# Sliding-window attention beside a gated MLP: the band in pieces of 64 queries, with shared columns for the half-masked ends

## The chip, the core and the metric

The kernel runs on one core of one Trainium2 chip. The metric is the device time of an execution in microseconds (us), lower is better; runs of the same kernel agree within a few tenths of a microsecond. The engines are named as in the profile: PE (matmuls), PEld (its weight loads), DVE (vector), ACT (activations), POOL (GpSimd), SP (the engine that issues most DMAs).

## The reference, cut to what matters

```python
x = A_x                                   # 1 x 2048 x 512, bf16
xn = layernorm(x)
# A: attention, 32 heads of 16, each query sees itself and the 255 keys before it
q, k, v = split_heads(xn @ wqkv)          # 512 -> 3 x 32 x 16
mask = (i - j >= 0) & (i - j < 256)
a = softmax(where(mask, q k^T * 16 ** -0.5, -1e9)) v
A = merge_heads(a) @ wo
# B: gated MLP with a mixing over the tokens
z = gelu(xn @ w_in)                       # 512 -> 2 x 688
z1, z2 = z[:, :688], layernorm(z[:, 688:])
g = w_sp @ z2 + b_sp[:, None]             # w_sp is 2048 x 2048
out = x + A + (z1 * g) @ w_out
```

## The kernel before

There are 2048 tokens in 16 row blocks of 128, and 32 heads in 4 groups G of 8. All order is written out by hand: each engine executes its instructions in the order in which the Python emits them.

**Stage one** (to about 54 us) loops over the row blocks. For block n it normalizes x (`stats` on DVE with a power on POOL, `norm` on DVE into the tile xn), transposes xn into `xnT`, and runs two groups of matmuls `do_z` (L285) whose results ACT turns into `z1_all` and `z2_all` with the Gelu (L293); DVE then normalizes z2. The first X_DMA = 8 blocks are transposed on PE (`transpose_x`, L274, with an ACT copy), the others by a DMA that SP issues (L265). From n = 5 on, one projection for head group 0 goes with each block (`early`: k, q and v of token groups 0 to 2, evicted by ACT); the last of them, v of group 2, goes with n = 14. x, w_in, wqkv, wo and w_out are loaded on SP's queue near the start, wo and w_out (L331 to L335) right after the last x block. N_WARM sets how many matmuls on zeros go ahead of the first work on PE.

**The band stage** executes a list of tokens, ORDER, one after the other:
- `pkGg`, `pqGg`, `pvGg` (capital P: another PSUM bank): the projection of head group G for 512 tokens g, on PE, evicted by DVE. k is kept twice, each copy with one half of each pair of heads set to zero (`emask`); a v tile has the layout [v of even heads, ones, v of odd heads], so one matmul gives both the output and the softmax sum.
- `qIIe`: scores of tile II for parity e. The band has 45 blocks of 128 keys x 128 queries for each head group (a key block kb meets query blocks kb, kb+1, kb+2), in the order of key blocks, 4 blocks to a tile: 45 tiles for the 4 groups. For each of the 4 head pairs s, a matmul on 32 rows of the array (32 x 128 tile form) takes the keys as weights and up to 384 queries as moving columns into the bank of strip s (L483). Then ACT takes two exponentials of 128 x 1024 into the tile E (L491), scaled.
- `mII`: masks on E. On blocks with kb = qb POOL's affine_select (L502) drops the keys after the query; on blocks with qb = kb+2 DVE multiplies by `fmask` (L507).
- `aGw`, `AGw` (and the pair `C`, `B`): values. For 256 queries w, 4 matmuls side by side on 32 columns each (128 x 32 tile form, L531) per key block, query block and parity; DVE transposes the result in 32 x 32 blocks, takes the reciprocal of the sums, POOL multiplies (`divide`). `t`: DVE transposes the attention output back (`finish`, L565).
- a number n: n matmuls of the token mixing, w_sp times z2 (`mix`, L402, 512 in all: 16 row blocks x 2 halves x 16 steps), with DVE's product with z1 after each 16. w_sp arrives transposed by DMA, one row block at a time into two buffers (`load_wsp`, L386, on SP's queue; the first two are issued ahead of the token list).
- `o`, `O`: half of a row block's output (L433 for wo, L439 for w_out), a DVE sum, and a DMA to the output, on SP's queue but for the last three blocks, which go on ACT's.

Score tiles, projections with P and outputs with O share three PSUM buffers of two banks (`ps_s`); another bank (`ps_y`) serves projections, values and outputs, and one the mixing. The k, q and v tiles live in rings of NRING = 6, the E tiles in EBUFS = 7 buffers.

## Time and profile before

The runs took 267.82, 267.84 and 267.96 us (median 267.84). The profiled execution took 268.1 us; its span, from the first to the last instruction, is 266.1 us.

| stretch (us) | PE busy | DVE busy | ACT busy | POOL busy |
|---|---|---|---|---|
| 0 to 20 (start of stage one) | 18.0 | 16.2 | 11.7 | 8.2 |
| 20 to 55 (stage one) | 34.7 | 29.4 | 24.9 | 13.6 |
| 55 to 90 (band) | 34.3 | 24.1 | 35.0 | 15.4 |
| 90 to 130 (band) | 39.4 | 31.7 | 39.6 | 22.4 |
| 130 to 170 (band) | 39.7 | 33.2 | 36.6 | 21.5 |
| 170 to 210 (band) | 39.8 | 29.3 | 35.0 | 24.2 |
| 210 to 242 (band, outputs) | 31.6 | 21.6 | 22.6 | 12.8 |
| 242 to 266.1 (mixing, outputs) | 20.9 | 11.7 | 0.5 | 5.4 |

Busy time is the union of an engine's instructions in the stretch. Matmuls overlap one another, so the busy time of PE says that it was never without one, not that the array was full; what an instruction of PE costs is the distance from its start to the next one's. The granted clock is 1.00 in every stretch.

### The profile page before, as it was taken

The numbers are of one execution on the slowest core, as the hardware profiler recorded it, in microseconds if no ns is written. First come the engines' busy times: TensorE is split into PE (matmuls) and PEld (weight loads), VectorE is DVE, ScalarE is ACT, GpSimd is POOL, SyncE is SP. The second block draws the span as 40 slices with busy tenths as digits, with TensorE's granted clock in tenths as the row PEclk, the third lists the DMA queues.
The fourth block names the chain that finished last, engine by engine and source line by source line (L and its number), as shares of the span: only waits on it lengthen the run. The fifth ranks groups of instructions, "written<-read, shape, count | busy, mean of one in ns | idle before, by whom it ended". The sixth has DMA issues, their size and how long they took to land.

```text
span 266.1 us, 8418 instructions
## 1 busy us (share of the span) xinstructions
PE 258.6 (97%) x3661; PEld 147.1 (55%) x3694; DVE 197.3 (74%) x384; ACT 206.0 (77%) x235; POOL 123.6 (46%) x140
## 2 busy tenths in 40 slices
PE   7999999999999999999999999999999999999995
PEld 2565665645455547554656656655665454554543
DVE  5999999567766778968788888767777658568542
ACT  3677767699999999999999899897899789553000
POOL 4334454115645256746637493156573617247200
PEclk9999999999999999999999999999999999999999
DMA  6992325700504050251312054033059972423733
GB/s 204 350 363 55 61 40 112 88 2 2 110 15 98 2 111 21 63 46 38 81 31 52 17 66 81 2 81 83 15 130 272 143 123 59 98 74 30 150 91 89
DMA packets 60132, 23.63 MB, mean 89 GB/s; under 512 B 51216, under 2 KB 59584, under 8 KB 60096
## 3 DMA queue, kind: packets, MB, share of 16 engines
q1 hardware_dynamic: 59472, 22.70, 38.5%
q8 instruction: 29, 0.48, 0.7%
q10 hardware_dynamic: 576, 0.39, 0.5%
q0 software_dynamic: 48, 0.00, 0.3%
q14 instruction: 7, 0.06, 0.1%
HBM read 8.41 MB, written 2.10 MB: 39 GB/s over the span
## 4 chain that ended last, share of the span: by engine, by line
PE 88%; ACT 7%; DMA 2%; issue 1%; SPq 1%; DVE 0%; ACTq 0%
PE gf L402 28%; PE zs L285 14%; PE S L483 11%; PE m L151 8%; PE o_t L531 8%; PE fo L439 8%; ACT E L491 7%; PE m L135 5%; PE fo L433 5%; DMA w_in_sb<-in_B_w_in_dram 2%; PE tp L274 1%; ACT L491 0%; DVE xnT L444 0%; SPq L194 0%; SPq L196 0%
## 5 line engine op out<-in xcount | busy, mean ns | idle before, releaser
L491 ACT ACTIVATE E<-S 128x1024 bf16<-128x1024 f32 x180 | 168.4, 1056 | 18.1 <-PE S L483 14.1
L402 PE MATMUL gf<-z_all,wspT 128*128 128x344 bf16 x512 | 94.2, 310 | 0.0
L502 POOL TENSOR_SCALAR_AFFINE_SELECT E<-E 128x1024 bf16<-128x1024 bf16 x64 | 79.3, 1264 | 18.1 <-ACT E L491 18.0
L402 PEld LDWEIGHTS <-wspT 128*128 128x128 bf16 x512 | 44.2, 98 | 33.8 <-issue 10.5
L554 POOL TENSOR_TENSOR o_norm<-o_c,rsum 128x256 bf16<-128x256 f32 x32 | 23.2, 726 | 77.3 <-DVE rsum L552 77.3
L507 DVE TENSOR_TENSOR E<-E,fmask 128x1024 bf16<-128x1024 bf16 x56 | 51.9, 954 | 1.6 <-ACT E L491 1.5
L285 PE MATMUL zs<-w_in_sb,xnT 128*128 128x176 bf16 (+1 forms) x250 | 39.7, 307 | 0.7 <-DMA w_in_sb<-in_B_w_in_dram 0.4
L483 PE MATMUL S<-q,k 32*128 32x128 bf16 (+2 forms) x888 | 38.5, 251 | 0.8 <-ACT E L491 0.8
L293 ACT ACTIVATE z_all<-zs 128x688 bf16<-128x688 f32 x32 | 23.8, 744 | 12.5 <-PE zs L285 12.5
L151 PE MATMUL m<-xnT,wqkv 128*128 128x512 bf16 x110 | 31.3, 379 | 0.9
L285 PEld LDWEIGHTS <-xnT 128*128 128x128 bf16 x256 | 22.2, 98 | 15.3 <-issue 0.6
L409 DVE SCALAR_TENSOR_TENSOR z_all<-gf,b_all,z_all 128x344 bf16<-128x344 f32 x32 | 18.2, 570 | 15.8 <-PE gf L402 15.7
L483 PEld LDWEIGHTS <-k 32*128 32x128 bf16 x888 | 15.2, 92 | 25.7 <-issue 23.7
L548 DVE STREAM_TRANSPOSE o_c<-o_t 128x512 f32<-128x512 f32 x32 | 22.3, 698 | 8.2 <-PE o_t L531 8.0
L531 PE MATMUL o_t<-E,v 128*32 128x128 bf16 x1440 | 24.5, 220 | 0.0
L531 PEld LDWEIGHTS <-v 128*32 128x32 bf16 x1440 | 20.3, 97 | 6.2 <-issue 6.0
L439 PE MATMUL fo<-w_out_sb,uT 128*128 128x512 bf16 (+2 forms) x98 | 23.0, 366 | 0.3 <-issue 0.2
L444 DVE TENSOR_TENSOR xnT<-fo,xnT 128x512 bf16<-128x512 f32 (+2 forms) x17 | 11.1, 657 | 13.6 <-PE fo L439 13.6
L171 DVE TENSOR_TENSOR k<-m,emask 128x1024 bf16<-128x1024 f32 x13 | 15.8, 1219 | 6.3 <-PE m L151 6.3
L151 PEld LDWEIGHTS <-wqkv 128*128 128x128 bf16 x128 | 12.0, 98 | 11.3 <-issue 0.9
L120 POOL TENSOR_TENSOR rstdx<-rs_v,negh 128x1 f32<-128x1 f32 x16 | 10.3, 646 | 16.1 <-DVE rs_v L119 14.7
L298 DVE BATCH_NORM_STATS2 st<-z_all 128x6 f32<-128x344 bf16 x32 | 14.9, 506 | 3.7 <-ACT z_all L293 3.7
(51 smaller groups left out, 177.4 us busy)
## 6 DMA issues: line engine op xcount, KB each, us to landing
xnT<-in_A_x_dram SPq DMA_DIRECT2D x4, 512.0 KB, 6.4
xs<-in_A_x_dram SPq DMA_DIRECT2D x7, 256.0 KB, 7.5
out_dram<-xnT SPq DMA_DIRECT2D x13, 128.0 KB, 1.7
wqkv<-in_A_wqkv_dram SPq DMA_DIRECT2D x1, 1536.0 KB, 7.2
w_in_sb<-in_B_w_in_dram SPq DMA_DIRECT2D x4, 344.0 KB, 5.1
w_out_sb<-in_B_w_out_dram SPq DMA_DIRECT2D x1, 640.0 KB, 10.4
wo_sb<-in_A_wo_dram SPq DMA_DIRECT2D x1, 512.0 KB, 9.1
xs<-in_A_x_dram SPq DMA_DIRECT2D x2, 128.0 KB, 2.1
```

Of the source, the lines that this page charges most:

```text
L151: nc.tensor.matmul(m, lhsT=wqkv[:, c, w0 : w0 + P], rhs=xnT[:, c, grp * 512 : (grp + 1) * 512], start=(c == 0), stop=(c == NDC - 1),)
L285: nc.tensor.matmul(zp[:, lo:hi], lhsT=xnT[:, c, n * P : (n + 1) * P], rhs=w_in_sb[:, c, f0 + lo : f0 + hi], start=(c == 0), stop=(c == NDC ...
L293: nc.scalar.activation(out=dst[:, n, 0:FH], in_=zp[:, 0:FH], func=ACT.Gelu_apprx_tanh)
L402: nc.tensor.matmul(gf[:, 0:FQ], lhsT=wsp_tiles[n][:, c, :], rhs=z2_all[:, c, lo : lo + FQ], start=(c == 0), stop=(c == NB - 1),)
L439: nc.tensor.matmul(fo[:, c0:c1], lhsT=uT_tiles[n][:, c, :], rhs=w_out_sb[:, c, c0:c1], start=False, stop=(c == NFC - 1),)
L483: nc.tensor.matmul(S[:, h2, j * P : (j + w) * P], lhsT=k_t[(G, kb // 4)][32 * s : 32 * s + 32, e, (kb % 4) * P : (kb % 4 + 1) * P], rhs=q_ ...
L491: nc.scalar.activation(out=E[:, j : j + 3 : 2, 0:nb, :].rearrange("p h b c -> p h (b c)"), in_=tiles[pr][:, :, 0 : nb * P], func=ACT.Exp, ...
L502: nc.gpsimd.affine_select(out=E[:, :, j, :], in_=E[:, :, j, :], pattern=[[0, 8], [1, P]], compare_op=ALU.is_ge, fill=0.0, base=0, channel_ ...
L507: nc.vector.tensor_tensor(out=E[:, :, j, :], in0=E[:, :, j, :], in1=fmask[:].unsqueeze(1).to_broadcast([P, 8, P]), op=ALU.mult,)
L531: nc.tensor.matmul(T[32 * s : 32 * s + 32, e, j * P : (j + 1) * P], lhsT=v_t[(G, kb // 4)][:, kb % 4, s, e : e + 2, :].rearrange("p a d -> ...
L548: nc.vector.transpose(out=C[:, 0 : 32 * DH], in_=Tb)
L554: nc.gpsimd.tensor_tensor(out=o_n[:], in0=c_o.rearrange("p e q d -> p q e d"), in1=rsum[:].rearrange("p e q -> p q e").unsqueeze(3).to_bro ...
```

## The change

The band is cut into pieces of 64 queries. A key block kb of 128 keys now meets queries in 64-query steps u: the steps 2kb+1 to 2kb+4 are pieces "F" (all 128 keys against 64 queries; the first still needs the causal mask, the last the far mask). The two ends of a band, step 2kb, of which only the first 64 keys are seen, and step 2kb+5, of which only the last 64 keys are, are each half of a piece. A piece "C" puts both in the same 64 columns: step 2kb of key block kb on the partitions 0 to 63, and step 2(kb-2)+5 of key block kb-2 on the partitions 64 to 127. That makes 304 pieces for the four head groups, 8 to a tile: 38 score tiles.

- A scores matmul now has 64 keys as weights (32 x 64 tile form): each piece takes 8 matmuls, 4 head pairs s times 2 key halves h; runs of F pieces of one key block go together, up to 256 columns. The loop runs over the pieces first, then s and h.
- The values of a C piece need v with its other half at zero: `w_bufs`, zeroed by POOL in stage one, filled from the v tile by two DMAs on SP's queue for each v projection. The value matmuls take runs of 64 to 192 queries, and only the first of a bank opens the accumulation.
- Masks: POOL's affine_select on 64 columns for the first F piece; DVE products on 64 columns for the last F piece (`fmask`) and for each C piece (`cmask`).
- NRING 6 to 5, EBUFS 7 to 6, X_DMA 8 to 6, N_WARM (9, 3) to (10, 3). The second half of w_in's first part is loaded ahead of the second x block. wo and w_out are loaded after the loop of stage one instead of near the start. In the last block, the first 384 output columns go on SP's queue. The token list is a new one.

```diff
-NRING = 6
-EBUFS = 7
-X_DMA = 8
+NRING = 5
+EBUFS = 6
+X_DMA = 6
-N_WARM = (9, 3)
+N_WARM = (10, 3)
-BLOCKS = [
-    [(G, kb, qb) for kb in range(NB) for qb in range(kb, min(kb + 3, NB))] for G in range(NG)
+PIECES = [
+    (G,) + p
+    for G in range(NG)
+    for kb in range(NB)
+    for p in [("C", kb, 2 * kb)]
+    + [("F", kb, u) for u in range(2 * kb + 1, min(2 * kb + 5, 2 * NB))]
 ]
-TILES = [b[i : i + 4] for b in [sum(BLOCKS, [])] for i in range(0, len(b), 4)]
+TILES = [PIECES[i : i + 8] for i in range(0, len(PIECES), 8)]
...
 ORDER = """
-pq10 Pk03 q000 1 pq03 2 q001 4 pk10 q010 9 m00 q011 pv11 m01 4 q020 4 pk11 q021 8 q030 a00 7
...
+pv03 q000 16 q001 pk03 3 q010 1 m00 8 q011 pq03 4 q020 pv10 m01 3 q021 1 a00 4 q030 8 m02 q031
+pk11 2 m03 2 q040 5 a01 q041 3 Pq12 a02 q050 4 t pk10 t q051 m04 8 q060 pq11 2 t 1 q061 5 pk12
+q070 2 m05 6 q071 a03 Pv11 4 m07 q080 pq10 4 q081 m06 a04 6 q090 4 t 6 m08 q091 a05 4 q100 2 m09
...
@@ proj @@
+            for h in range(2):
+                nc.sync.dma_start(out=wt[64 * h : 64 * h + 64, h], in_=t[64 * h : 64 * h + 64])
...
         load_x(0, split=True)
         load_win(1, 0, 2)
+        load_win(1, 2, 4)
         load_x(1)
-        load_win(1, 2, 4)
...
@@ small_setup @@
             if i < NRING:
                 nc.gpsimd.memset(v_bufs[i][:, :, :, 1, :], 1.0)
+                nc.gpsimd.memset(w_bufs[i][:], 0.0)
...
         for n2 in range(4, NB // 2):
             load_x(n2)
-        nc.sync.dma_start(out=wo_sb[:], in_=A_wo.rearrange("(c p) n -> p c n", p=P))
-        nc.sync.dma_start(
-            out=w_out_sb[:, 0:5, :], in_=B_w_out[0:640, :].rearrange("(c p) n -> p c n", p=P)
-        )
-        nc.sync.dma_start(out=w_out_sb[0 : FH - 5 * P, 5, :], in_=B_w_out[5 * P : FH, :])
...
             do_z(n - 1, 0)
+        nc.sync.dma_start(out=wo_sb[:], in_=A_wo.rearrange("(c p) n -> p c n", p=P))
+        nc.sync.dma_start(
+            out=w_out_sb[:, 0:5, :], in_=B_w_out[0:640, :].rearrange("(c p) n -> p c n", p=P)
+        )
+        nc.sync.dma_start(out=w_out_sb[0 : FH - 5 * P, 5, :], in_=B_w_out[5 * P : FH, :])
...
@@ out_part @@
-        (nc.scalar if n >= NB - 3 else nc.sync).dma_start(
+        (nc.scalar if n >= NB - 3 and c1 == D else nc.sync).dma_start(
...
@@ scores @@
-                for j, G, kb, qb, w in segs:
+        for j, G, kind, kb, u, w in segs:
+            for s in range(4):
+                for h in range(2):
+                    if kind == "F":
+                        ku, qu = 2 * kb + h, u
+                    else:
+                        ku, qu = 2 * (kb - 2 * h if kb >= 2 else kb) + h, u + h
                     nc.tensor.matmul(
-                        S[:, h2, j * P : (j + w) * P],
-                        lhsT=k_t[(G, kb // 4)][32 * s : 32 * s + 32, e, (kb % 4) * P : (kb % 4 + 1) * P],
-                        rhs=q_t[(G, qb // 4)][32 * s : 32 * s + 32, (qb % 4) * P : (qb % 4 + w) * P],
+                        tiles[s // 2][64 * h : 64 * h + 64, s % 2, 64 * j : 64 * (j + w)],
+                        lhsT=k_t[(G, ku // 8)][32 * s : 32 * s + 32, e, (ku % 8) * 64 : (ku % 8 + 1) * 64],
+                        rhs=q_t[(G, qu // 8)][32 * s : 32 * s + 32, (qu % 8) * 64 : (qu % 8 + w) * 64],
                         start=True, stop=True,
                     )
...
@@ masks @@
+            part = E[:, :, 64 * j : 64 * j + 64]
+            if kind == "F" and u == 2 * kb + 1:
                 nc.gpsimd.affine_select(
+                    out=part, in_=part, pattern=[[0, 8], [1, 64]],
+                    compare_op=ALU.is_ge, fill=0.0, base=64, channel_multiplier=-1,
                 )
+            elif kind == "C" or u == 2 * kb + 4:
+                m = cmask if kind == "C" else fmask
                 nc.vector.tensor_tensor(
+                    out=part, in0=part,
+                    in1=m[:].unsqueeze(1).to_broadcast([P, 8, 64]), op=ALU.mult,
                 )
...
@@ values @@
+        steps = [(e,) + tuple(r) for e in range(2) for r in runs(places)]
+        for n, (e, (kind, kb), i, j, u, l) in enumerate(steps):
+            for s in range(4):
+                vt = w_t if kind else v_t
+                vv = vt[(G, kb // 4)][:, kind - 1] if kind else vt[(G, kb // 4)]
+                nc.tensor.matmul(
+                    T[32 * s : 32 * s + 32, e, (u - 4 * w) * 64 : (u - 4 * w + l) * 64],
+                    lhsT=vv[:, kb % 4, s, e : e + 2, :].rearrange("p a d -> p (a d)"),
+                    rhs=E_tiles[i][:, 2 * s + e, 64 * j : 64 * (j + l)],
+                    start=(n == 0), stop=(n == len(steps) - 1), skip_group_check=True,
+                )
```

## The prediction

> **What bounds the kernel now.** I read the page first, for which engine is full and where.

> ```profile
> span 266.1 us, 8418 instructions
> ...
> PE 258.6 (97%) x3661; PEld 147.1 (55%) x3694; DVE 197.3 (74%) x384; ACT 206.0 (77%) x235; POOL 123.6 (46%) x140
> ...
> PE   7999999999999999999999999999999999999995
> ...
> ACT  3677767699999999999999899897899789553000
> ```

> PE is full in every slice between the first and the last; ACT is full only in the first half of the band stage. The list of waits asks whether that full PE ever waits inside:

> ```profile
> PE S L483 <- ACT E L491: 0.8, 3, 0.3
> ```

> Three waits, 0.8 us. So time is PE's own instructions, and the change is first a change in PE's sum. The groups give what it touches:

> ```profile
> L491 ACT ACTIVATE E<-S 128x1024 bf16<-128x1024 f32 x180 | 168.4, 1056 | 18.1 <-PE S L483 14.1
> ...
> L502 POOL TENSOR_SCALAR_AFFINE_SELECT E<-E 128x1024 bf16<-128x1024 bf16 x64 | 79.3, 1264 | 18.1 <-ACT E L491 18.0
> ...
> L507 DVE TENSOR_TENSOR E<-E,fmask 128x1024 bf16<-128x1024 bf16 x56 | 51.9, 954 | 1.6 <-ACT E L491 1.5
> ```

> The mean of a pipelined matmul isn't its price; the distance between starts is. The timeline of PE shows it (start, length, count last):

> ```profile
> 130.13 1.06 PE L135 MATMUL m<-wqkv,xnT 128*128 128x128 bf16 x16
> 131.02 1.04 PE L402 MATMUL gf<-z_all,wspT 128*128 128x344 bf16 x6
> 131.99 0.41 PE L483 MATMUL S<-q,k 32*128 32x128 bf16 x8
> 132.33 0.85 PE L531 MATMUL o_t<-E,v 128*32 128x128 bf16 x48
> 133.13 0.60 PE L402 MATMUL gf<-z_all,wspT 128*128 128x344 bf16 x3
> ```

> Sixteen matmuls of 128 columns take 0.89 us, 0.0556 each; four of 512 (56.14 to 57.00) 0.215 each. So a column costs 0.415 ns and a matmul 2.5 ns more: 0.145 us for 344 columns, 0.029 for 64. Six of 344 from 131.02 end at 131.89, yet the scores start at 131.99: a change of tile form (128*128, 32*128, 128*32) costs 0.10. The 48 value matmuls take 0.80 = 12 sets of four at 0.0556, plus 0.10 for the next change and 0.03; so four strips run together, their weight loads hidden. The scores take 0.34: 512 columns (0.213), two pieces (0.005), a change (0.10), and 0.02 of strips starting in turn. With four pieces it is 0.36 (125.73 to 126.09).

> Last, the start of the band stage, since the order and the queues change there:

> ```profile
> 49.28 0.58 ACT L145 CAST v<-m 128x512 bf16<-128x512 f32 x1 [0.15 <-PE m L135]
> ...
> 53.75 1.89 PE L151 MATMUL m<-xnT,wqkv 128*128 128x512 bf16 x8
> ```

> and SP's queue, at the same place and at the one other place where a transpose stands behind large loads:

> ```profile
> 43.14 5.89 SPq L386 DMA_TRANSPOSE wspT<-in_B_w_sp_dram  x2
> ...
> 196.78 3.39 SPq L578 DMA_DIRECT2D xnT<-in_A_x_dram  x4
> 200.28 6.23 SPq L386 DMA_TRANSPOSE wspT<-in_B_w_sp_dram  x1
> ```

> SP issues the first two w_sp transposes from 43.14; the first lands 4.5 us later, at 47.6, long before the first mix matmul (55.91). At 200.28 a transpose issued behind four 512 KB loads of the same queue is held by them for 6.23 us and lands after 9.8.

> **PE's sum.** Counts come from the instruction order of both kernels. Scores: 90 groups become 76. Columns per strip go from 184320/4 to 311296/8, 46080 to 38912, matmuls per strip from 222 to 352: 19.7 to 17.0 us, −2.65. Form changes fall from 206 to 181: −2.5. The starting of strips: eight instead of four, up to five pieces; I take 0.05 for the 0.03 of now, 76×0.05 against 90×0.03: +1.1 (bounds −1 and rival B). Values: the same columns in 2048 matmuls for 1440, 152 more sets of four at 2.5 ns: +0.4 (0 to rival B). Together −3.65.

> **Stage one.** Two row blocks leave PE's transposes for DMA: 8×0.0556, −0.45. Their DMAs are needed at about 22.6 us; each takes 2.4 us (as the others) from xn written by about 18.3, behind x loads landing until about 19: no wait. w_in's second half goes ahead of the second x load. Now PE waits 0.43 us for w_in at 7.72, and the x block lands at 5.92 (2.20 + 3.7). Swapped, that x lands where w_in lands now, 7.68, 1.75 later. From that x to xn of block 2 takes 2.7 us (5.92 to 8.60), so 10.2, and PE, which now reaches that transpose at 9.47 and otherwise would at 8.9, waits: +0.75 against now (0 to 1.0). The tenth warm-up matmul ends at 5.49 against xn at 5.40: +0.05. The memsets of the w buffers (POOL's 640-element one takes 0.63, so about 1.5 each) fall in POOL's idle time before rstd (15 us); if not, DVE's xn is 2 us ahead. The first 384 output columns of the last block go through SP's queue, so the last transfer no longer queues behind them: −0.15 (0 to −0.4).

> **The queue.** wo and w_out, loaded at 11 to 22 us now, move behind stage one, ahead of the w_sp transposes on SP. So do two copies for each v projection, which wait for ACT's or DVE's copy of v. The last early v projection is evicted at 49.28+0.58 = 49.86, and stage one ends 0.35 later than now (0.75+0.05−0.45), so 50.2. Behind it SP issues two copies, wo, w_out in two parts (0.45 each, as its x loads): the first w_sp transpose cannot be issued before 52.4; now it is at 43.14. It lands at 52.4+4.5 = 56.9 at the earliest. But 1.2 MB stand before it: wo issued at 51.1, data from 1.75 later (the first 128 KB x load: 2.1 to landing, 0.37 of it transfer), at 0.35 MB/us (1.5 MB of wqkv in 4.5 us), done at 56.3. At 200 us the transpose landed at 210.07, 3.4 after the last load (206.66): 59.7. And the new order asks for it sooner: one v projection, one score group, then 16 mix matmuls. Stage one's last matmul ends at 53.75+0.35 = 54.1; +0.89+0.10+0.36 = 55.45. PE is in order, so all of PE stands behind that mix: 59.7−55.45 = **+4.3 us**, at least 56.9−55.45 = 1.4, at most about 5. The second transpose, some 5.3 later (47.6 and 53.0 now), comes at 65; PE needs it at about 69. In an idle spell of over 4 us the clock may fall: the page's PEclk never shows it in the band, but the first nine 128x512 matmuls run at 0.427 each against 0.215 later, 1.9 us lost; that is an end of the range. [...]

> **Other engines.** ACT: 152 exponentials for 180 at 0.936 (168.4/180): 142 us for 168, so PE's 0.8 us of waits mostly goes: −0.5. POOL: 64 masks of half size. DVE gets 120 mask products of 512 elements for 56 of 1024; the row of that line runs from 0.63 to 1.61 us (the long ones beside POOL's masks), mean 0.93. Half is 0.46; I take 0.5 (0.35 to 0.65): 60 us for 52. Per head group DVE then has 10.4 (k, q, v copies) + 15.0 + 11.0 (eight divisions) + 4.6 (mix) = 41 of PE's 43; now 39 of 47. At 95% some of PE's banks come free late: +0.8 (0 to 4).

> The smaller rings (five k, q, v and w buffers, six E tiles) cost nothing where the order emits a projection after the last value group that reads the buffer it takes (Pv11 stands after a02); the mix matmuls between are the cover, and a miss would cost PE one value group, under 1 us.

> **Sum.** −3.65−0.45+0.75+0.05−0.15+4.3−0.5+0.8 = +1.15. The profiled execution took 268.1, 2.0 over its span; 269.25. The median of the runs, 267.84, lies 0.26 lower: 269.0.

> **Rivals.**
> A, faster: the w_sp transpose is there nearly in time. If loads and transpose shared the 16 DMA engines, it would land at 56.9, PE would wait 1.4: 266.1; without any wait 264.7. For: engines do work side by side, and SP's copies are small. Against: the 6.23 us above. It decides from landing at 58 downward. 0.24.
> B, narrow strips are dear: no set in the trace is narrower than 128 columns. If a set of 64 score columns is held up by its next weights, it takes up to the 0.0556 of now instead of 0.029: 1728/8 = 216 sets, +5.7: 274.7; with the values' 392 sets too, +10.4 more; were only four of the eight strips to run together, +17. Against: loads are hidden today at two in the time of one. 0.12. [...]
> C, DVE becomes the bound in the middle (products at 0.65): 120×0.15 = 18 us more, PE waits some 4: 272.2. 0.10.

> **Numbers.** My forecast has 0.54; its own range is 266.8 to 271.5. Within 0.2% (about what a measurement can tell) is ±0.54. From the forecast come 0.05 faster, 0.13 same, 0.36 slower; A gives 0.23 faster and 0.01 same; B and C 0.22 slower. The range takes in A, C and the clock: 265.7 to 272.8.

> **What would show it.** PE's first mix waits on DMA wspT for 3.5 to 5 us near 55; score groups start-to-next 0.36 to 0.38 on PE; no DVE releaser over 1 us in PE's waits; the tail unchanged. It is wrong if w_sp lands before 57, if a score group takes over 0.42, or if PE waits for DVE by several us.

## The result: slower by an eighth, against a forecast of half a per cent

The changed kernel took 301.61 us (median of four runs, 299.72 to 306.35), the kernel before 267.83 beside it: a ratio of 1.1239, 95% interval 1.1187 to 1.129. The forecast was 269.0, with a range to 272.8. The direction was right, the size far off. The profiled execution took 299.72 us. Every ratio here leaves out disturbed executions (of these four, the one of 306.35 us), so it is not quite the quotient of the medians.

The page of the changed kernel, its lines for the span, the engines, PE's slices, the granted clock and the instruction queue:

```profile
span 298.0 us, 13620 instructions
...
PE 266.9 (90%) x6223; PEld 163.7 (55%) x6223; DVE 210.6 (71%) x449; ACT 182.2 (61%) x205; POOL 95.1 (32%) x147
...
PE   8999889659999889897999699979797969799995
...
PEclk9999999959999999999999979999999999999999
...
q8 instruction: 48, 0.79, 1.2%
```

The span grew by 31.9 us. PE's row of nines is gone: its busy time grew by 8 us, its share fell from 97% to 90%. No other engine is fuller than 71%, so nothing else has become the bound. The two counts to look at are x6223 + x6223 instructions on PE (before 3661 + 3694), and 48 packets on queue q8, which carries instructions, of 16 KB each. The page of the kernel before has 29 of them:

```profile
q8 instruction: 29, 0.48, 0.7%
```

The list of waits of the changed kernel names what PE waited for (total, times, longest):

```profile
PE S L520 <- issue: 8.3, 5, 2.5
...
PE o_t L575 <- issue: 6.9, 7, 2.0
...
PE gf L440 <- DMA wspT<-in_B_w_sp_dram: 6.2, 1, 6.2
...
PE zs L323 <- DMA xnT<-xn: 2.3, 2, 1.2
...
PE m L154 <- issue: 2.1, 1, 2.1
...
PE gf L440 <- issue: 0.6, 1, 0.6
```

"issue" means that nothing in the profile released the engine: no semaphore, no DMA of data. PE's timeline shows such a stop in the middle of a score group, 40 matmuls with no wait among them (start, length, count last; in brackets the idle time):

```profile
198.08 0.60 PE L440 MATMUL gf<-z_all,wspT 128*128 128x344 bf16 x3
198.61 0.54 PE L520 MATMUL S<-q,k 32*64 32x128 bf16 x35
201.24 0.28 PE L520 MATMUL S<-q,k 32*64 32x192 bf16 x5 [2.09 <-issue]
...
236.13 0.51 PE L520 MATMUL S<-q,k 32*64 32x64 bf16 x40
236.57 1.05 PE L440 MATMUL gf<-z_all,wspT 128*128 128x344 bf16 x6
```

The gaps were read from the trace's raw rows: 13 of them lose over half a microsecond each, 19.8 us together, the longest 2.7. Count PE's rows (matmuls and weight loads): all 13 come at row 190 of a run of 256, and q8 brings one packet of 16 KB for every 255 to 259 of these rows (7,390 over 29 packets in the kernel before, 12,448 over 48 in the changed one), so that a packet is read here as one such run. At all 13, PE goes on 1.2 to 1.5 us after the end of a q8 packet: at the gap of 201.24 the packet runs from 198.94 to 199.90, at 241.32 from 238.99 to 240.04. In the kernel before, the shortest block of 256 between these rows lasted 4.26 us, 25 of 28 lasted over 6, and no gap stands at any border. In the changed one 23 of 47 blocks last under 3.8 us. All 13 gaps stand behind blocks of 1.3 to 3.6 us and none behind a longer one; of the ten other short blocks, nine lasted 3.4 us or more.

Where the 31.9 us went: 19.8 gaps at these borders; 6.3 the first mix's wait for w_sp; 2.6 the two waits for xnT in stage one; 3.3 at half clock (6.8 us granted at 0.5 from 59.7, of which PE ran 3.2, and 3.4 from 172.3). That is 32.0, so what is left of the change's own sum nearly cancels; this rest was not measured by itself.

The last two lines of that timeline show a second thing: a score group without a stop takes 0.44 us from its start to the next matmul (236.13 to 236.57). The mean over such groups is 0.437, where 0.375 was expected.

### The profile page after: what moved, and what is told of

It reads as the page before. It is cut to its first block, busy times and chain, and to the rows that moved or that the text cites. A ratio compares the mean times of both kernels' runs of the same rounds, so it can differ in the third digit from the quotient of the medians.

```text
span 298.0 us, 13620 instructions
## 1 busy us (share of the span) xinstructions
PE 266.9 (90%) x6223; PEld 163.7 (55%) x6223; DVE 210.6 (71%) x449; ACT 182.2 (61%) x205; POOL 95.1 (32%) x147
## 4 chain that ended last, share of the span: by engine, by line
PE 71%; DVE 14%; issue 7%; DMA 5%; SPq 2%; POOL 0%; ACT 0%; DVEq 0%
PE gf L440 26%; PE S L520 11%; PE m L174 8%; PE o_t L575 8%; PE fo L477 7%; PE fo L471 5%; PE m L154 4%; DVE st L292 3%; DMA wspT<-in_B_w_sp_dram 2%; DVE st L336 2%; DVE xn L298 2%; PE zs L323 2%; DVE E L543 2%; DMA xs<-in_A_x_dram 1%; DVE z_all L342 1%
## 5 line engine op out<-in xcount | busy, mean ns | idle before, releaser
L528 ACT ACTIVATE E<-S 128x1024 bf16<-128x1024 f32 x152 | 145.5, 1024 | 64.2 <-PE S L520 56.3
L440 PEld LDWEIGHTS <-wspT 128*128 128x128 bf16 x512 | 45.5, 99 | 33.9 <-DMA wspT<-in_B_w_sp_dram 6.3
L537 POOL TENSOR_SCALAR_AFFINE_SELECT E<-E 128x512 bf16<-128x512 bf16 x64 | 47.1, 760 | 27.3 <-ACT E L528 27.3
L520 PE MATMUL S<-q,k 32*64 32x64 bf16 (+3 forms) x2816 | 39.5, 217 | 8.3 <-issue 8.3
L520 PEld LDWEIGHTS <-k 32*64 32x64 bf16 x2816 | 27.9, 105 | 30.7 <-issue 29.8
L323 PE MATMUL zs<-w_in_sb,xnT 128*128 128x512 bf16 (+1 forms) x256 | 40.1, 309 | 2.3 <-DMA xnT<-xn 2.3
L543 DVE TENSOR_TENSOR E<-E,cmask 128x512 bf16<-128x512 bf16 x64 | 37.9, 599 | 0.0
L591 DVE STREAM_TRANSPOSE o_c<-o_t 128x512 f32<-128x512 f32 x32 | 22.6, 707 | 17.4 <-PE o_t L575 16.1
L543 DVE TENSOR_TENSOR E<-E,fmask 128x512 bf16<-128x512 bf16 x56 | 30.3, 542 | 0.1
L575 PE MATMUL o_t<-E,v 128*32 128x64 bf16 (+2 forms) x1088 | 23.6, 215 | 4.4 <-issue 4.3
L575 PE MATMUL o_t<-E,w 128*32 128x64 bf16 x960 | 19.0, 193 | 2.6 <-issue 2.6
L154 PE MATMUL m<-wqkv,xnT 128*128 128x128 bf16 x256 | 17.6, 222 | 2.1 <-issue 2.1
```

Of the source, the lines that this page charges most:

```text
L154: nc.tensor.matmul(m[:, j * P : (j + 1) * P], lhsT=xnT[:, c, n * P : (n + 1) * P], rhs=wqkv[:, c, 2 * D + G * P : 2 * D + (G + 1) * P], st ...
L323: nc.tensor.matmul(zp[:, lo:hi], lhsT=xnT[:, c, n * P : (n + 1) * P], rhs=w_in_sb[:, c, f0 + lo : f0 + hi], start=(c == 0), stop=(c == NDC ...
L440: nc.tensor.matmul(gf[:, 0:FQ], lhsT=wsp_tiles[n][:, c, :], rhs=z2_all[:, c, lo : lo + FQ], start=(c == 0), stop=(c == NB - 1),)
L520: nc.tensor.matmul(tiles[s // 2][64 * h : 64 * h + 64, s % 2, 64 * j : 64 * (j + w)], lhsT=k_t[(G, ku // 8)][32 * s : 32 * s + 32, e, (ku ...
L528: nc.scalar.activation(out=E[:, j : j + 3 : 2, :], in_=tiles[pr][:], func=ACT.Exp, scale=SM_SCALE)
L537: nc.gpsimd.affine_select(out=part, in_=part, pattern=[[0, 8], [1, 64]], compare_op=ALU.is_ge, fill=0.0, base=64, channel_multiplier=-1,)
```

## The experiments

Two theories were tested. **One**: PE's instructions come in blocks of 256, a block takes a few microseconds to come, and the change, with 1.7 times the instructions for the same matrix work, runs PE out of them. **Its rivals**: narrow sets are dear in themselves (B of the prediction), or the gaps are waits for other engines or for traffic. Beside that, the three smaller losses were taken apart.

### e1: narrow matmuls in the kernel before

Each score and value matmul is cut to at most 64 columns; nothing else changes.

```diff
@@ scores, inside "for s" @@
-    nc.tensor.matmul(S[:, h2, j * P : (j + w) * P], ...)
+    for c in range(0, w * P, 64):
+        nc.tensor.matmul(S[:, h2, j * P + c : j * P + c + 64], ...)
```

> The kernel before, with each score and value matmul cut into matmuls of 64 columns (same tile forms, same order of tokens, same queues): 7127 matmuls' worth of PE instructions in place of 3695, 14254 rows in place of 7390. Theory 1 (PE's instructions arrive in blocks of 256, some 4 us after the block before is entered, and PE stands at a block's border where 256 instructions last less than that): idle PE marked 'issue' of 1 to 3 us at borders 256 instructions apart, 15 to 35 us in all, 283 to 303 us, although no piece is in the 32 x 64 form and nothing else has changed. Theory 2 (the gaps belong to the new tile form, the w copies or the new order): only the 2.5 ns of each further matmul and the emptying queue, 1 to 5 us more, 269 to 273 us, and no gap of a microsecond marked 'issue'.

Measured: 349.82 us, ratio 1.288 (1.279 to 1.2969), far above the 283 to 303 expected. 31 us lie in 18 gaps at block borders, the longest 5.2. But the edit brought a second effect: with eight narrow pieces of one strip in a row, the four strips overlapped only in part, and a score group took 0.74 where it takes 0.35, some 35 us over 90 groups. And 37.5 us of the profiled execution ran at half clock. So the gaps are there with none of the change's pieces, masks or copies, but the total doesn't isolate them. e5 repairs that. The "emptying queue" of the second theory is the author's assumption; no run shows it.

### e5: the same, with the strips innermost

```diff
-    for pr, h2 (strip s) ... for j, G, kb, qb, w in segs:
+    for j, G, kb, qb, w in segs:
+        for c in range(0, w * P, 64):
+            for s in range(4):
```

> The kernel before, with nothing changed but that every score and value matmul is cut into pieces of 64 columns, the strips innermost: as many columns and as many multiplications as before, about twice the PE instructions (some 14,250 rows for 7,390). Theory one (TensorE's instructions are delivered in blocks of 256, and a block takes 2.5 to 6 us to come, so that it stands where 256 instructions last less): gaps marked issue at block borders of 20 to 40 us in all, 290 to 315 us. Rival (the narrow sets themselves, or the new masks and forms of the change, cost the time, not the number of instructions): no gaps at the borders, score groups of 0.35 to 0.40 us, 268 to 275 us.

Measured: 324.81 us, ratio 1.2092 (1.2016 to 1.2167), beyond the upper end of the expectation. PE's timeline and the waits of e5:

```profile
244.56 0.39 PE L480 MATMUL S<-q,k 32*128 32x64 bf16 x13 [5.48 <-issue]
...
270.27 0.41 PE L480 MATMUL S<-q,k 32*128 32x64 bf16 x32
270.62 0.60 PE L439 MATMUL fo<-w_out_sb,uT 128*128 128x512 bf16 x2
```

```profile
PE S L480 <- issue: 19.1, 11, 5.5
...
PE o_t L528 <- issue: 16.9, 9, 3.8
```

The undisturbed group from 270.27 takes 0.35 us, as before with half as many pieces (0.34 to 0.36): cutting the sets cost the array nothing. All the loss is outside: 41.1 us in 22 gaps, and 27 us in seven spells of half clock beside gaps, up to 13.6 us more. Together that is up to 54.7 of the span's 55.0. Work, columns, masks and loads are those of the kernel before; the number of PE instructions is not, nor is the order of the strips inside a group, which the group of 0.35 us shows to cost nothing. That is theory one, and it excludes the rival that narrow sets are dear in themselves, and any that needs the change's form, masks or copies.

### e8: the supply by itself

1,024 matmuls of 64 columns behind the last output, when no other engine works.

```diff
+    spare = ps_g.tile([P, 512], F32, name="spare", tag="g")
+    for i in range(1024):
+        s = i % 4
+        nc.tensor.matmul(spare[32 * s : 32 * s + 32, 0:64], lhsT=ident[:, 32 * s : 32 * s + 32],
+                         rhs=wo_sb[:, 0, 0:64], start=True, stop=True)
```

> The kernel before with 1,024 matmuls of 64 columns by 32 rows of output added behind its last output (work that nothing reads; 2,048 PE instructions), four strips in turn, no wait among them. It measures the supply by itself, with no other engine at work. If TensorE had its instructions at once they would take 1,024 x 7.3 ns = 7.5 us. Theory one: eight blocks of 256 at 2.5 to 4 us each, one gap in each at a 256 border, 20 to 30 us more than before. Rival (the gaps come from waits for other engines that the trace does not show): 8 to 12 us more, no gaps.

Measured: 293.06 us, ratio 1.0947 (1.0914 to 1.0981), 25 us more, as theory one has it. PE's timeline:

```profile
263.81 2.17 PE L600 MATMUL spare<-wo_sb,ident 128*32 128x64 bf16 x241
268.31 1.22 PE L600 MATMUL spare<-wo_sb,ident 128*32 128x64 bf16 x128 [2.33 <-issue]
272.03 1.90 PE L600 MATMUL spare<-wo_sb,ident 128*32 128x64 bf16 x128 [2.51 <-issue]
...
282.94 1.90 PE L600 MATMUL spare<-wo_sb,ident 128*32 128x64 bf16 x128 [1.56 <-issue]
```

Bursts of 128 matmuls (256 instructions with their weight loads) start every 3.45 to 3.73 us, whether the burst itself takes 1.2 us or, at half clock, 1.9. So the period is set by the delivery, not by PE, with almost no other traffic (0.25 MB in the 27 us from 264 to 291, seven q8 packets for the seven gaps among it). The rows show its parts: the q8 packet starts 0.95 to 1.16 us after PE has entered the block that goes before, takes 0.93 to 1.36, and PE goes on 1.23 to 1.47 us after its end. At the changed kernel's borders the same period (256 instructions and the gap behind them) is 3.1 to 5.8 us, for example 1.31 + 1.86 and 3.07 + 2.70. There the packet starts 0.1 to 3.4 us after the block is entered, and the four gaps of over 2 us stand behind packets that start 2.4 us after it or later; what makes these late is not shown.

### e4: fewer instructions in the change

The F pieces' scores in the 32x128 form (one matmul for 128 keys instead of two for 64); C pieces behind them. 10,656 PE instructions instead of 12,448.

```diff
-        for j, G, kind, kb, u, w in segs:
+        for j, G, kind, kb, u, w in sorted(segs, key=lambda x: x[2] == "C"):
...
+                if kind == "F":
+                    nc.tensor.matmul(tiles[s // 2][:, s % 2, 64 * j : 64 * (j + w)],
+                        lhsT=k_t[...][32 * s : 32 * s + 32, e, (kb % 4) * P : (kb % 4 + 1) * P], ...)
+                    continue
```

> The changed kernel with the scores of the F pieces taken by whole key blocks (32 x 128 form, one matmul where there were two), the C pieces after them in the 32 x 64 form: PE rows fall from 12448 to 10656, and each score group has one more change of form (76 x 0.1 = 7.6 us). Theory 1: score groups fit in the queue again and blocks of 256 last longer: the gaps marked 'issue' fall from 20 us to 5 to 10, groups are not longer than before by more than the 0.1: 290 to 298 us. If the gaps have nothing to do with the number of instructions, they stay at 20 and the change of form adds 5 to 8: 304 to 310 us.

Measured: 287.56, 288.37, 293.11 and 503.15 us, ratio 1.074 (1.0719 to 1.0762) from the first two. The execution of 503.15 us is the profiled one; its matmuls ran at little more than half the speed (0.259 us from one of 344 columns to the next for 0.146, not a third as the next expectation says), its cause is open, and its profile is not used. A further run gave another:

> The kernel of e4 once more, for a profile whose gaps can be read: the first one's profiled execution ran at a third of the speed throughout. Theory one: 10,656 rows for 12,448, gaps at block borders of 8 to 14 us for 20, the F part of a score group 0.16 us or more shorter or no hole in its pairs, about 287 to 291 us.

288.7 us, with these waits:

```profile
PE gf L440 <- DMA wspT<-in_B_w_sp_dram: 6.8, 1, 6.8
PE o_t L580 <- issue: 4.1, 4, 1.9
PE zs L323 <- DMA xnT<-xn: 2.1, 3, 1.3
...
PE S L525 <- issue: 0.9, 1, 0.9
PE gf L440 <- issue: 0.6, 1, 0.6
```

The border gaps fell from 19.8 to 6.2 us, within the 5 to 10 first expected and under the 8 to 14 of the second expectation; the total fell by 13 us; the waits for w_sp and xnT stayed. A score group did not get shorter: F and C parts together take 0.474, since the change of form between them costs its 0.10 (131.89 to 131.99 in the kernel before). So the time was saved by the smaller number of instructions, not by the form. That a score group must fit in a queue, as the first expectation has it, is the author's assumption; no run shows it.

### e2 and e3: the late loads

e2 is the changed kernel with wo and w_out loaded where they were before; e3 is the kernel before with the change's side edits (x blocks 6 and 7 by DMA, ten warm-up matmuls, w_in's second half ahead of the second x block, late wo and w_out, the split output queue) and nothing of the band.

```diff
@@ e2, against the changed kernel @@
         for n2 in range(4, NB // 2): load_x(n2)
+        (the three DMAs of wo and w_out)
...
             do_z(n - 1, 0)
-        (the three DMAs of wo and w_out)
```

> The changed kernel with the loads of wo and w_out back at their old place, right after the x loads. If the 6.4 us for which the first mix waits on the w_sp transpose come from those loads standing ahead of it, the wait falls to 0 to 1.5 us (the transpose still stands behind the last v copy, 50 us) and with it the spell at half clock after it: 6 to 8 us less than the changed kernel, 293 to 295 us. If the v copies alone held the transpose, the wait stays over 3 us: 298 to 301 us. The gaps marked 'issue' stay at some 20 us under either.

Measured: 297.38 us, ratio 1.1113 (1.1065 to 1.1162): 4 us less than the changed kernel, where 6 to 8 were expected. PE's waits in e2:

```profile
PE zs L323 <- DMA xnT<-xn: 2.7, 1, 2.7
...
PE gf L440 <- DMA wspT<-in_B_w_sp_dram: 0.8, 1, 0.8
```

The wait for w_sp fell from 6.3 to 1.0 us (0.8 in the list, which leaves out the change of form), so the late loads are its cause. But the waits for xnT did not get smaller: in place of the two of 2.6 us in all stands one of 2.9 at 24.9 us, since the DMA transposes of x blocks 6 and 7 now stood behind those loads, and a wait of 0.7 for xn stands at 9.8 us. The gaps (19.1) stayed.

> The kernel before with the side edits alone (6 blocks transposed on PE for 8, ten warm-up matmuls, w_in's second half ahead of the second x block, wo and w_out loaded behind stage one, last block's first output part on SP's queue): no change of the band, no v copies. My sum for these edits: -0.45 for the transposes, +0.8 for the x block, -0.15 for the output, and no wait for w_sp, since without v copies its transpose is issued at about 44 us and lands at 51 to 52, before the first mix at 56: 267.5 to 268.5 us. If the late loads alone delay the mix, 270 to 274 us. If the DMA transposes of blocks 6 and 7 come late by themselves, 0.5 to 3 us more and waits on xnT in stage one.

Measured: 267.65 us against 268.04, ratio 0.9982 (0.997 to 0.9995), and no new wait on PE. Without the w copies and the late xn, SP reaches the first w_sp transpose at 45.5 us there, behind the same late loads, where the changed kernel reaches it at 56.07. The side edits alone are a small gain. Nothing else that was run came under the kernel before.

### e6: without the w copies

The waits for xnT in stage one were put down to SP, whose transposes of xn stand behind copies of v that wait for ACT. e6 leaves the copies out; the C values read the whole v tile, so this kernel's output is another, and only its time is of use.

```diff
-            for h in range(2):
-                nc.sync.dma_start(out=wt[64 * h : 64 * h + 64, h], in_=t[64 * h : 64 * h + 64])
...
-                vv = vt[(G, kb // 4)][:, kind - 1] if kind else vt[(G, kb // 4)]
+                vv = v_t[(G, kb // 4)]
```

> The changed kernel without the half-zeroed copies of v (the values of the C pairs read the whole v tile, so the other half is not left out of their sum), that is without the DMAs that wait on SP for ACT's copy of v. Theory one: the two waits for xnT in stage one (2.6 us) go, the wait of the first mix for w_sp falls from 6.3 to 2 to 4 us since SP comes to the late loads earlier, the 20 us of gaps at block borders stay: 293 to 297 us. Rival (the block borders' gaps come from these copies' traffic): gaps under 10 us, under 288 us.

Measured: 291.59 us, ratio 1.088 (1.0864 to 1.0896), less than the 293 to 297 expected. Two parts of the expectation failed. The waits for xnT stayed, 0.91 and 1.36 us raw for 1.23 and 1.38: the copies were not their cause. The wait for w_sp fell to 3.3, as expected. The gaps fell only from 19.8 to some 16 us, so the copies account for at most some 4 us of them, and aren't why blocks are late.

### e9 and e11: the zeroing

The trace then showed what held xn up: DVE's own instruction. DVE's and POOL's timelines of the changed kernel in stage one:

```profile
30.79 1.56 DVE L298 TENSOR_SCALAR xn<-xs,mvx,rstdx 128x512 bf16<-128x512 bf16 x1
...
33.35 1.53 DVE L342 TENSOR_SCALAR z_all<-z_all,mv,rstd 128x688 bf16<-128x688 bf16 x2
```

```profile
30.83 1.38 POOL L272 MEMSET w<- 128x1536 bf16 x1
...
32.95 1.38 POOL L272 MEMSET w<- 128x1536 bf16 x1
```

The xn instruction takes 0.41 us elsewhere. It starts beside POOL's zeroing of a w buffer and ends just after it (32.21 and 32.36); SP issues the transpose at 32.38, and PE, waiting for it, goes on at 35.53. The batch statistics that DVE runs beside a zeroing are not stretched (0.69 us at 23.11, beside the zeroing from 23.17, as without one; 0.50 at 32.70); the bf16 TENSOR_SCALAR instructions are (xn 1.56 for 0.41 twice, z_all 1.17 for 0.41 twice). e9 takes the zeroing away from there; e11 adds such a zeroing to the kernel before.

```diff
@@ e9, against the changed kernel @@
+        nc.vector.memset(w_bufs[0][:], 0.0)                 # ahead of the first x block
+        nc.scalar.copy(out=w_bufs[1][:] ..., in_=zeros[:] ...)
...
-                nc.gpsimd.memset(w_bufs[i][:], 0.0)
+            elif i < NRING + 6:                             # three later steps of the set-up
+                nc.gpsimd.memset(w_bufs[i - NRING - 1][:], 0.0)
@@ e11, against the kernel before @@
                 nc.gpsimd.memset(v_bufs[i][:, :, :, 1, :], 1.0)
+                nc.gpsimd.memset(spare[:], 0.0)             # 128 x 1536 bf16, read by nothing
```

> The changed kernel with the zeroing of the five w buffers taken out of stage one's middle: one on DVE and one on ACT ahead of the first x block, three on POOL after the other set-up. Taking the w copies away (e6) left the two waits for xnT as they were, so those copies do not cause them. New theory: POOL's zeroing (1.38 us each) holds DVE's bf16 instructions up (xn took 1.56 us where it takes 0.41, z_all 1.17 for 0.41, three times beside a zeroing), DVE then hands xn over late, and PE waits. It expects no xn or z_all instruction of DVE over 1 us between 25 and 42 us, no wait for xnT over 0.5 us in stage one, the first mix's wait for w_sp and the 20 us of gaps at block borders as they were: 2 to 3 us less than the changed kernel, about 297 to 299 us. Rival (DVE has too much to do in stage one, whatever POOL does): waits for xnT of 2 us or more stay, no gain.

> The kernel before with five zeroings of a spare 1,536-element buffer on POOL at the places where the changed kernel has them (nothing reads the buffer). Theory (POOL's zeroing holds DVE up): some xn or z_all instructions of DVE take 1.0 to 1.6 us instead of 0.41, each beside a zeroing, xnT is late by as much, and PE waits 0.5 to 3 us in stage one: 268.3 to 271 us. Rival (the zeroing costs nothing as the prediction had it): no DVE instruction stretched, 267.8 to 268.2 us.

e9, the xn line's summary between 20 and 50 us (min, median, max in ns):

```profile
L304 DVE TENSOR_SCALAR xn<-xs,mvx,rstdx x9: 402/412/570, 20.1 to 44.3; 128x512 bf16<-128x512 bf16 x9
```

No xn is stretched, PE's waits for xnT are gone, and the first mix starts at 59.75 instead of 63.30. The total doesn't show it: 294.35 to 300.79 us over four runs where 297 to 299 were expected, ratio 1.1058 (1.0964 to 1.1152); the profiled one had five spells of half clock where the changed kernel's had two. For the end of the kernel e9 is inconclusive, for stage one it is clear. The cleaner total is e11's: 270.05 us, ratio 1.0074 (1.0057 to 1.0091), with the expected stretch and wait:

```profile
37.16 1.57 DVE L262 TENSOR_SCALAR xn<-xs,mvx,rstdx 128x512 bf16<-128x512 bf16 x1
...
39.72 1.52 DVE L306 TENSOR_SCALAR z_all<-z_all,mv,rstd 128x688 bf16<-128x688 bf16 x2
```

```profile
PE zs L287 <- DMA xnT<-xn: 1.3, 2, 0.8
```

By what the zeroing holds DVE up is not shown. The trace of the changed kernel has 1.56 us for 0.41 beside a zeroing of 1.38, with an end 0.15 us after the zeroing's; which of the two came first it doesn't settle, since DVE's row starts 0.04 us ahead of POOL's.

### e7 and e10: the repairs together

e7 is e4 with the early loads, all of the first eight x blocks on PE again, and the first w copies on ACT's queue; e10 adds e9's zeroing.

```diff
-X_DMA = 6
+X_DMA = 8
...
-                nc.sync.dma_start(out=wt[64 * h : 64 * h + 64, h], in_=t[64 * h : 64 * h + 64])
+                (nc.scalar if on_act else nc.sync).dma_start(out=wt[64 * h : 64 * h + 64, h], in_=t[64 * h : 64 * h + 64])
```

> The changed kernel with the F scores in strips of 32x128 with all their columns in one matmul (10,656 PE rows for 12,448), the C scores as they were, the attention's output weights loaded where the kernel before loads them, no x block left to the late DMAs, and the first w copies on ACT's queue. Theory one: no wait for w_sp or xnT over 1 us, gaps at block borders of 8 to 14 us for 20, 276 to 284 us. Rival (the waits of stage one and two only move to the next one late): 286 us or more.

> e7_combined with the zeroing moved as in e9: 282.1 us there; theory: its waits for xnT (1.8 us) go, the gaps at block borders (about 8 us) stay: 279 to 281 us. Rival: 282 us or more. All of the changed kernel's own saving is then weighed against the kernel before with the waits of stage one out of the way; what is left over 268 should be gaps at block borders and score groups.

Measured: 282.11 us, ratio 1.052 (1.0497 to 1.0542), and 279.48, ratio 1.0428 (1.0396 to 1.046). PE's waits in e10:

```profile
PE o_t L588 <- issue: 3.5, 3, 1.7
PE S L533 <- issue: 1.7, 2, 1.3
PE gf L448 <- issue: 1.6, 2, 1.4
...
PE tp L320 <- DVE xn L306: 1.1, 2, 0.7
```

The waits for DMA are gone, e7's 1.8 us for xnT too; 1.1 us of waits for xn remain at the start. Of the 13.1 us that e10's span is still longer, 7.9 are gaps at borders, up to 1.7 a spell of half clock, and 4.9 the score groups (76 x 0.477 = 36.3 us for 90 x 0.349 = 31.4); the rest comes to −1.4. In the changed kernel's own form the groups take 76 x 0.437 = 33.2 us, also more than 31.4. So even with the waits repaired the saved score tiles are not a saving on PE.

## Why the prediction was right in sign and wrong in size

**PE's sum (predicted −3.65): the step that failed.** It priced a matmul by the distance between starts, which holds while PE has its instructions. That price was right for sets of four strips: in e5, a score group of 64-column sets takes 0.345 us, as the wide ones did. But the step multiplied it by counts without asking whether so many instructions arrive. The count was in the prediction (352 score matmuls in each of eight strips, 2,816, for 222 in each of four, 888; 2,048 value matmuls for 1,440), and the page's q8 line was there to be read. No row of the trace of before shows the limit, since its shortest block of 256 instructions lasted 4.26 us and most over 6; a density of instructions beyond any seen there was an unknown, and should have had bounds. Cost: 19.8 us of gaps, and 1.7 us of half clock behind one of them. The block is read from the runs: all 13 gaps lie 256 rows apart or a multiple of it, q8's packets have 16 KB, and in e8 one packet comes with each burst of 256. The shortest period was 3.1 us; why it is that long, and how many blocks PE holds, no run here settles.

**Score groups (predicted 0.375 us, mis-sized by 4.7 us in all).** They took 0.437 on average, above the 0.42 that the prediction named as a sign of being wrong. Groups of 32 matmuls take 0.367, as predicted; the 40-matmul ones 0.44 to 0.52. In these, after 32 matmuls and their loads (64 instructions) the loads have a hole of about 0.1 us, and then the rest comes at about 8 ns a matmul. That reading rests on the rows of groups of both sizes; it was not tried by itself, and the cause stays open.

**The queue (predicted +4.3, measured 6.3).** The mechanism, the place and the releaser were right: PE's first mix on wspT, with all of PE behind it. e2 shows that the late loads are the cause. The size failed in two terms. SP reached the first w_sp transpose at 56.07 us instead of 52.4, since stage one ended later and the w_out load alone kept SP 1.88 us where 0.45 was taken:

```profile
51.80 1.10 SPq L170 DMA_DIRECT2D w<-v  x2
52.95 0.58 SPq L401 DMA_DIRECT2D wo_sb<-in_A_wo_dram  x1
53.58 1.88 SPq L402 DMA_DIRECT2D w_out_sb<-in_B_w_out_dram  x1
...
56.07 6.57 SPq L424 DMA_TRANSPOSE wspT<-in_B_w_sp_dram  x2
```

It landed at 63.25, not 59.7, and PE asked for it at 56.9 instead of 55.45.

**Stage one (predicted +0.35 in sum).** The cover for the zeroing failed: "fall in POOL's idle time" was true of POOL and said nothing of DVE. It cost 2.6 us of waits here and 1.9 of e11's total. The fallback, "DVE's xn is 2 us ahead", was too little for two stretched instructions in a row. The +0.75 for the swapped x block had the wrong sign: PE reaches that transpose at 9.21 us, after a wait of 0.25, where 10.2 was forecast and the kernel before has 9.47. Without the zeroing the side edits are a gain: e3 has −0.4 us in all where the terms gave +0.2.

**Other engines.** DVE did not become the bound: in none of PE's waits over 0.3 us in the band does it stand as the releaser, and rival C is out. The +0.8 for it was not needed.

**Rival B** is out as well: 64-column sets run at 29 ns in scores and values, and eight strips run together. A weight load's row lasts some 0.1 us in the changed kernel (105 ns in the scores, 96 in the values), yet the sets go on every 29 ns: the loads of the strips hide beside one another, and e5's groups show no cost (0.345 us). **Rival A** is out by 6.3 us.

**The clock.** The end of the range for it was named and came: half clock from 59.7, 2.8 us into the wait for w_sp, 1.6 us lost while PE ran, where 1.9 was taken. That "an idle spell of over 4 us" is needed was not shown: a gap of 2.2 us at 171.14 also brought a spell, and others of 2.3 and 2.7 us none. That was not foreseen, and the rows show the pattern. The two spells last 6.827 and 3.413 us in the trace's records of the granted clock, and the full clock between them 105.813, 31 times 3.413. They start at 59.70 and 172.34, which is 33 steps of 3.413 us apart. Counted in such steps, PE was without a matmul for 75% and 100% of the two steps from 56.29 and for 58% of the one from 168.93, and each time the step after ran at half clock. No other step of the band has over 53%, and none brought a spell: the gap of 171.14 lies in one step, those of 2.3 (201.24) and 2.7 us (241.32) are each split over two. In e9 four gaps of 1.9 to 2.4 us, 51 to 64% of a step, brought spells, and a step of 52% did not, so in these two runs the limit lies near half a step. Whether such a gap costs 1.7 us more hangs on where it falls, which is luck here. Why a spell lasts is not explained by this: one in e1 went on for six steps, and in the last five of them PE stood for 14% or less.

## What to carry to other kernels

Count PE's instructions as well as its columns: matmul and weight load each are one, and here 256 of them should last 4 us or more (about 16 ns each), or PE stands at the block's border. That mark is rough: in the changed kernel no gap follows a block of over 3.6 us, in e1 and e5 one each, of about half a microsecond, follows blocks of 4.5 and 4.8. Cutting matmuls finer so as to skip masked columns pays only while that holds. And "this engine is idle then" is no cover for a moved instruction before it is asked which other engine's work it holds up (here the zeroing of 1.38 us, with DVE's xn at 1.56 us for 0.41) and what stands behind it in its queue.
